# A fused attention and feed-forward kernel: low parts last in the first m-tile, two blocks in halves, another VectorE order in the bursts, a split last store

## The chip, the cores and the metric

The kernel runs on one core of a Trainium2 chip. The metric is device time in microseconds (us) from start to end of one execution; lower is better. The engines are called as the profile calls them: PE is TensorE (matmuls; PEld its weight loads), DVE is VectorE, ACT is ScalarE, POOL is GpSimd, SP is SyncE, which issues the DMAs.

## The reference

```python
# q, k, v: (8, 8, 576, 64) f32; attention inside chunks of 64 rows
scores = 1/sqrt(64) * q_c @ k_c.T            # per batch, head, chunk
attn   = exp(scores - max); attn = attn / (sum(attn) + 1e-9)
x      = (attn @ v_c) -> (4608, 512)         # heads side by side
h      = x @ w_in                            # w_in (512, 2048)
g      = maximum(h, 0) + log1p(exp(-abs(h))) # softplus
out    = g @ w_out                           # w_out (2048, 512), out (4608, 512) f32
```

## The kernel before

**Tiles.** The 4608 rows are 36 tiles of 128 (two chunks of one or two batches); four tiles are an m-tile of 512 rows, so there are 9 m-tiles. The hidden width of 2048 is 16 blocks of 128 (fc). For each m-tile and block, `gemm1` (L558) makes a 128x512 PSUM tile of h: 12 matmuls. `sp_g` (L578, ACT) is the softplus into u, `sp_hi` (L582, ACT) rounds it to g_hi, `sp_lo` (L586, DVE or POOL) makes g_lo = u − g_hi, and `gemm2` (L592) adds its product with w_out to four PSUM tiles: 12 matmuls. That is 9 × 16 × 2 = 288 groups of 12.

**Parts.** Each f32 operand is split into a high part, rounded to fp32r, and a low rest. A product is three matmuls: low times high, high times low, high times high, in that order before (L568, L601). The weights come as raw f32; per unit u (512 columns of w_in or w_out, 32 units) a DMA (`load`), a cast of the top (`w_top`, ACT or POOL), a scaled copy of the bottom (`w_low`, ACT), an addition (`w_add`, DVE), the high cast (`w_hi`, ACT or POOL) and the subtraction (`w_lo`, DVE or POOL) make the two parts.

**Attention.** The first four tiles (blocks 0 to 3) go through transposes on PE (`pe_t`, `pe_s`, `pe_e`, `pe_v`). From block 4 on two blocks go at a time, in 17 **bursts**: a burst (L550) does for each of two blocks the product with v of the pair before (`blk_v`, L532) and the scores of the next pair (`blk_s`, L451), both into one two-bank PSUM buffer `pa`. There are two such buffers, and gemm1 uses them too: after a burst the next gemm1 needs the first burst buffer. A buffer is free when ACT has cast x's high part out of it (`att_xh`, L544), DVE has subtracted it for the low part (`att_xl`, L548), and DVE has taken the row maximum (`att_max`, L496) and subtracted it (`att_sub`, L501). Then exp (ACT), denominator, normalisation, a 32x32 transpose (`blk_e`) and a swap of quarters, by 8 DMAs on SP's queue (`blk_swap`) or by transposes of parts on DVE (`blk_e4`, blocks in SWAP_DVE). q and k are loaded either in 8 small DMAs each or in one or two (blocks in WHOLE); the second way needs 8 partial transposes per tensor on DVE (`blk_t4`) instead of one (`blk_t`).

**Order.** Each engine's instruction order is written by a planner, `Plan` (L34 to L144): every piece of work is a task with engine, assumed cost, needs, and an urgency; the planner simulates the engines and always takes the ready task with the lowest urgency number. `due(g)` = T0 + TG × g gives the urgencies of what block g needs. `needs` wait for the end of a task, `after` only for its issue. The costs steer only the order; on the chip the engines wait for each other's semaphores. PE's order is fixed (L800 to L808): gemm1 of a block, a burst if one stands at that block (BEGIN, BURST_AT), gemm2 of the block before. Block 0 of the first m-tile is done in two halves (HALVES = 1): tiles 0 and 1 ahead as `a0`, then tiles 2 and 3. `keep_warm` (L330) puts filler matmuls where the plan sees PE idle. At the end `evacuate` (L607) copies each of four 128x512 results to SBUF, in turn on ACT and DVE, and `store` (L614) writes it with a DMA on SP's queue.

## Time and profile before

| | us |
|---|---|
| median of 3 runs | 866.99 (866.23 to 867.52) |
| profiled execution, its own time | 869.51 |
| its span, first to last instruction | 867.7 |
| busy PE / DVE / ACT / POOL | 850.9 / 347.6 / 309.9 / 64.7 |

The page also cuts the span into 40 equal slices of 21.7 us, with busy tenths in each; 9 is 90% or more:

```profile
DVE  5999964333424161425232342334241614121111
ACT  4576744232423242424242332324232424232222
POOL 0564641000000000000000000000000000000000
```

PE is at 9 in all slices but three. DVE is at 9 from the second slice to the fifth, where weights, the first m-tile and the early attention blocks meet; POOL works in the first seven slices only.

### The profile page before, as it was taken

What the parts mean: (1) busy time and instruction counts of PE and PEld (TensorE: products, weight loads), DVE (VectorE), ACT (ScalarE), POOL (GpSimd) and SP (SyncE); (2) the same over time, 40 slices, a digit from 0 to 9 for tenths busy, and PEclk for the clock granted to TensorE, in tenths of its full rate; (3) what the DMA queues carried; (4) which work ended last, traced back from release to release, by engine and by line L of the source; (5) the groups of instructions that cost most, each with busy time, mean ns of one, the idle gap of its engine ahead of it and who ended that gap; (6) DMA issues with size and microseconds to landing.
All of it is one profiled execution on the core that took longest, in us unless ns stands there. A gap on an engine that the chain in (4) does not pass through costs nothing.

```text
span 867.7 us, 14820 instructions
## 1 busy us (share of the span) xinstructions
PE 850.9 (98%) x5874; PEld 701.5 (81%) x5874; DVE 347.6 (40%) x589; ACT 309.9 (36%) x483; POOL 64.7 (7%) x68
## 2 busy tenths in 40 slices
PE   8799999999999999999999999999999999999998
PEld 7677878888888888888888888888888888888886
DVE  5999964333424161425232342334241614121111
ACT  4576744232423242424242332324232424232222
POOL 0564641000000000000000000000000000000000
PEclk9999999999999999999999999999999999999999
DMA  9787763312242224131332223122422241000001
GB/s 225 189 213 211 181 152 86 68 38 52 42 100 40 53 40 108 33 66 28 72 74 49 48 45 98 40 51 42 100 39 55 39 103 37 18 22 27 1 1 48
DMA packets 209957, 63.65 MB, mean 73 GB/s; under 512 B 187104, under 2 KB 203232, under 8 KB 209888
## 3 DMA queue, kind: packets, MB, share of 16 engines
q1 hardware_dynamic: 209888, 62.71, 31.8%
q8 instruction: 46, 0.75, 0.4%
q14 instruction: 23, 0.19, 0.1%
HBM read 45.09 MB, written 9.44 MB: 63 GB/s over the span
## 4 chain that ended last, share of the span: by engine, by line
PE 88%; DMA 5%; DVE 4%; ACT 1%; issue 1%; SPq 1%; POOL 0%; DVEq 0%; POOLq 0%; ACTq 0%
PE pa L569 42%; PE po L602 42%; DMA raw<-in_moe_w_out_dram 3%; PE pa L532 2%; PE pa L451 1%; DMA raw<-in_moe_w_in_dram 1%; DMA eT<-ka 1%; DVE wib L263 1%; PE po L332 1%; DVE g_lo L588 0%; SPq L324 0%; ACT u L580 0%; DVE mx L496 0%; DVE low L263 0%; DMA k<-in_v_dram 0%
## 5 line engine op out<-in xcount | busy, mean ns | idle before, releaser
L580 ACT ACTIVATE u<-pa 128x512 f32<-128x512 f32 (+1 forms) x145 | 86.2, 594 | 500.3 <-PE pa L569 500.2
L569 PE MATMUL pa<-x,wib 128*128 128x512 f32 x864 | 208.1, 390 | 0.3
L588 DVE TENSOR_TENSOR g_lo<-u,g_hi 128x512 fp32r<-128x512 f32 (+1 forms) x137 | 95.2, 695 | 280.1 <-ACT g_hi L584 276.6
L569 PEld LDWEIGHTS pa<-x,wib 128*128 128x128 f32 x864 | 161.7, 188 | 36.0 <-PE po L602 2.6
L569 PE MATMUL pa<-x,wi_hi 128*128 128x512 f32 (+1 forms) x584 | 178.8, 388 | 2.1 <-DVE x L548 2.1
L602 PE MATMUL po<-late,g_hi 128*128 128x512 f32 x540 | 169.5, 390 | 0.0
L569 PEld LDWEIGHTS pa<-x,wi_hi 128*128 128x128 f32 x584 | 109.8, 189 | 24.3 <-DVE x L548 2.3
L602 PEld LDWEIGHTS po<-late,g_hi 128*128 128x128 f32 x540 | 101.2, 188 | 21.3 <-issue 0.5
L569 PE MATMUL pa<-x,wi_lo 128*128 128x512 f32 (+1 forms) x292 | 113.8, 390 | 1.6 <-POOL top L249 1.0
L602 PE MATMUL po<-wo_hi,g_lo 128*128 128x512 f32 x288 | 113.4, 394 | 0.0
L602 PE MATMUL po<-late,g_lo 128*128 128x512 f32 x288 | 113.0, 392 | 0.0
L602 PE MATMUL po<-wo_lo,g_hi 128*128 128x512 f32 x288 | 112.4, 390 | 0.0
L602 PE MATMUL po<-wo_hi,g_hi 128*128 128x512 f32 x288 | 112.4, 390 | 0.0
L584 ACT CAST g_hi<-u 128x512 fp32r<-128x512 f32 (+1 forms) x145 | 89.5, 618 | 4.4
L569 PEld LDWEIGHTS pa<-x,wi_lo 128*128 128x128 f32 x292 | 55.1, 189 | 15.3 <-PE po L602 3.3
L602 PEld LDWEIGHTS po<-wo_hi,g_lo 128*128 128x128 f32 x288 | 54.3, 189 | 11.7
L602 PEld LDWEIGHTS po<-late,g_lo 128*128 128x128 f32 x288 | 54.1, 188 | 11.6
L602 PEld LDWEIGHTS po<-wo_hi,g_hi 128*128 128x128 f32 x288 | 54.2, 188 | 11.3
L602 PEld LDWEIGHTS po<-wo_lo,g_hi 128*128 128x128 f32 x288 | 54.3, 189 | 10.9
L496 DVE TENSOR_REDUCE mx<-pa 128x8 f32<-128x512 f32 x32 | 21.9, 685 | 68.5 <-ACT x L544 68.0
L428 DVE STREAM_TRANSPOSE qe<-q 128x512 f32<-128x512 f32 x29 | 20.5, 705 | 70.6 <-DMA k<-in_k_dram 55.2
L428 DVE STREAM_TRANSPOSE ka<-k 128x512 f32<-128x512 f32 x29 | 20.6, 711 | 53.0 <-DMA k<-in_k_dram 33.5
(101 smaller groups left out, 564.1 us busy)
## 6 DMA issues: line engine op xcount, KB each, us to landing
out_dram<-raw SPq DMA_DIRECT2D x36, 256.0 KB, 2.4
raw<-in_moe_w_in_dram SPq DMA_DIRECT2D x16, 512.0 KB, 4.9
raw<-in_moe_w_out_dram SPq DMA_DIRECT2D x16, 512.0 KB, 5.1
eT<-ka SPq DMA_DIRECT2D x248, 32.0 KB, 1.9
q<-in_q_dram SPq DMA_DIRECT2D x232, 32.0 KB, 2.1
k<-in_k_dram SPq DMA_DIRECT2D x232, 32.0 KB, 2.1
q<-in_v_dram SPq DMA_DIRECT2D x60, 64.0 KB, 2.5
k<-in_v_dram SPq DMA_DIRECT2D x60, 64.0 KB, 2.5
```

The lines of the kernel that those rows point to most:

```text
L263: nc.vector.tensor_tensor(low, low, live.pop(("top", u)), op=ALU.add)
L332: nc.tensor.matmul(dst[:, :P], ident, ident, start=True, stop=True)
L428: nc.vector.transpose(t, live.pop((n, i)))
L451: nc.tensor.matmul(pa[o, c2, col : col + C], qT[r, a * HP + hl, :], kT[r, a * HP + hl, :], start=True, stop=True,)
L496: nc.vector.tensor_reduce(mx, sc, axis=AX.X, op=ALU.max)
L532: nc.tensor.matmul(pa[o, a, col : col + C], vt[r, 4 * j + 2 * h2 + c2, :], eT[r, :, 4 * c2 + 2 * j + h2, :], start=True, stop=True,)
L569: nc.tensor.matmul(ph, wt[:, c, fs], x[:, ts_, c, :], start=(n == 0), stop=(n == 3 * KC - 1))
L580: nc.scalar.activation(w["u"], w["ph"], AF.Softplus)
L584: nc.scalar.copy(w["hi"], w["u"])
L588: (nc.gpsimd if pool else nc.vector).tensor_tensor(w["lo"], w["u"], w["hi"].bitcast(F32), op=ALU.subtract)
L602: nc.tensor.matmul(pos[w["m"]][t], gg[:, ts_], wt, start=(w["first"] and n == 0), stop=(w["last"] and n == 2),)
```

## The change

1. In the first m-tile (m < 1) gemm1 and gemm2 do all high-times-high matmuls of a group first, then the other two kinds; later m-tiles keep the three kinds side by side, high times high first. The planner is told by `late` that w_lo, x_lo and g_lo are needed only later in such a group.
2. HALVES = 2: blocks 0 and 1 of the first m-tile are done in halves.
3. In a burst `max` is planned to follow its block's x high cast; the second block's max, and the second x subtraction, follow the issue of the first block's score subtraction.
4. The last 128x512 result is copied in two halves of 256 columns, on ACT and DVE, and stored by two DMAs, one on ACT's queue, one on SP's.
5. The planner's costs and its lists of what runs where are other numbers, so the order of the first m-tile is another; the bursts stand at blocks 5 and 13 of an m-tile instead of 6 and 14, and weight loads follow the issue of v3's load instead of v0's.

```diff
@@ Plan.add, Plan.order
+        late={}
-                r = max(r, fin[n] + lat)
+                r = max(r, fin[n] + lat - t["late"].get(n, 0.0))
...
@@ gemm1
-        n = 0
-        for c in range(KC):
-            for wt, x in ((wi_lo, x_hi), (wi_hi, x_lo), (wi_hi, x_hi)):
-                nc.tensor.matmul(
-                    ph, wt[:, c, fs], x[:, ts_, c, :], start=(n == 0), stop=(n == 3 * KC - 1)
-                )
-                n += 1
+        terms = ((wi_hi, x_hi), (wi_lo, x_hi), (wi_hi, x_lo))
+        order = [(c, t) for t in terms for c in range(KC)] if w["m"] < 1 else [(c, t) for c in range(KC) for t in terms]
+        for n, (c, (wt, x)) in enumerate(order):
+            nc.tensor.matmul(ph, wt[:, c, fs], x[:, ts_, c, :], start=(n == 0), stop=(n == 3 * KC - 1))
@@ gemm2
-        for j, t in enumerate(w["tiles"]):
-            ts_ = slice(j * P, (j + 1) * P)
-            for n, (gg, wt) in enumerate(((g_lo, w_hi_), (g_hi, w_lo_), (g_hi, w_hi_))):
-                nc.tensor.matmul(
-                    pos[w["m"]][t], gg[:, ts_], wt,
-                    start=(w["first"] and n == 0), stop=(w["last"] and n == 2),
-                )
+        terms = ((g_hi, w_hi_), (g_hi, w_lo_), (g_lo, w_hi_))
+        tiles = list(enumerate(w["tiles"]))
+        order = [(n, j) for n in range(3) for j in tiles] if w["m"] < 1 else [(n, j) for j in tiles for n in range(3)]
+        for n, (j, t) in order:
+            nc.tensor.matmul(
+                pos[w["m"]][t], terms[n][0][:, j * P : (j + 1) * P], terms[n][1],
+                start=(w["first"] and n == 0), stop=(w["last"] and n == 2),
+            )
@@ new
+    def last_half(w, j):
+        m, t = w["m"], TPM - 1
+        cols = slice(j * DM // 2, (j + 1) * DM // 2)
+        o = live["out", m, t // 2][:, DM + cols.start : DM + cols.stop].bitcast(F32)
+        (nc.vector.tensor_copy if j else nc.scalar.copy)(o, pos[m][t][:, cols])
+        (nc.sync if j else nc.scalar).dma_start(out[m * MT + t * P : m * MT + (t + 1) * P, cols], o)
@@ the lists
-    HALVES = 1
+    HALVES = 2
...
-    T0, TG = 28.0, 5.5
+    T0, TG = 14.0, 5.5
...
-    WHOLE = (4,7)
-    SWAP_DVE = (7,)
+    WHOLE = (4,7,9)
+    SWAP_DVE = (4,7,9)
-    TOP_ACT = (0,3,8,9,11,15,16,17,20,21,25,26,29)
-    LOAD_AFTER = "v0"
-    LO_POOL = (0,2,6,9,10,12,17,18,23,25,29,31)
-    NORM_POOL = (3,5,6,7)
-    GLO_POOL = (4,6,9,10,12,15,17,18)
+    TOP_ACT = (0,1,4,5,6,7,8,11,15,17,20,21,24,25,26,28,29,30)
+    LOAD_AFTER = "v3"
+    LO_POOL = (0,2,3,4,5,6,7,12,17,18,19,20,26,27,28,30,31)
+    NORM_POOL = (1,2,4,7)
+    GLO_POOL = (0,3,5,7,8,9,10,11,14,15,16)
-    BURST_AT = (6, 14)
+    BURST_AT = (5, 13)
-    V_AFTER = "load16"
-    K6_AFTER = "load10"
-    QK_URG = 30
+    V_AFTER = "load8"
+    K6_AFTER = "load13"
+    QK_URG = 0
-    V_URG = -5
-    SW_URG = 0
-    EXP_FROM = 1
+    V_URG = 20
+    SW_URG = 40
+    EXP_FROM = 3
...
@@ the bursts
-                plan.add(f"xl{i}", "DVE", 0.65, partial(att_xl, i), [f"xh{i}"], urg=d)
+                plan.add(f"xl{i}", "DVE", 0.65, partial(att_xl, i), [f"xh{i}"], urg=d + 0.5 * n,
+                         after=[f"sub{2 * ps}"] if n and ps is not None else [])
-            plan.add(f"max{i}", "DVE", 0.65, partial(att_max, i), [f"B{at}_{n}"], urg=d)
-            plan.add(f"sub{i}", "DVE", 0.65, partial(att_sub, i), [f"max{i}"], urg=d)
+            first = [f"B{at}_{n}"] if bursts[at][0] is None else [f"xh{2 * bursts[at][0] + n}"]
+            plan.add(f"max{i}", "DVE", 0.68, partial(att_max, i), first, urg=d + 0.2 * n,
+                     after=[f"sub{a}"] if n else [])
+            plan.add(f"sub{i}", "DVE", 0.68, partial(att_sub, i), [f"max{i}"], urg=d + 0.2 * n)
...
@@ the tasks of gemm1 and gemm2
+            slow = {f"w_lo{of_in[fc]}": 0.9 * part, **{f"xl{m * TPM + t}": 1.8 * part for t in w["tiles"]}}
+        slow = {f"w_lo{of_out[fc]}": 0.9 * part, f"lo{name}": 1.8 * part} if m < 1 else {}
...
@@ the last result
+                if m == NM - 1 and t == TPM - 1:
+                    for j in range(2):
+                        plan.add(f"ev{m}_{t}" + "ab"[j], "DVE" if j else "ACT", 0.4, partial(last_half, w, j), [f"G2_{g}"],
+                                 urg=-3, after=[f"ev{m}_{t - 1}"])
+                    continue
```

## Rows read from the trace of the kernel before

**Rows 1.** The page's chain that ended last, shares of the span by engine.

```profile
PE 88%; DMA 5%; DVE 4%; ACT 1%; issue 1%; SPq 1%; POOL 0%; DVEq 0%; POOLq 0%; ACTq 0%
```

**Rows 2.** Stages: stretch, its length, busy us (instructions) by engine, clock, DMA share, GB/s.

```profile
core 0: us, PE busy (x) PEld busy (x) DVE busy (x) ACT busy (x) POOL busy (x), PEclk, DMA share, GB/s
25.49:27.16 1.67, 1.67 (x12) 1.47 (x12) 1.60 (x5) 1.65 (x4) 0.60 (x1) 1.00 1.04 272
27.16:33.83 6.67, 3.45 (x54) 3.00 (x53) 6.60 (x11) 4.68 (x8) 4.22 (x5) 1.00 0.66 146
33.83:38.16 4.33, 4.33 (x17) 3.92 (x18) 4.24 (x8) 1.48 (x3) 0.87 (x3) 0.61 0.64 133
38.16:50.50 12.34, 12.34 (x56) 9.96 (x54) 11.54 (x20) 7.29 (x12) 6.74 (x8) 1.00 0.73 203
50.50:80.90 30.40, 29.11 (x185) 23.48 (x185) 27.78 (x47) 19.95 (x31) 16.74 (x17) 1.00 0.78 211
80.90:122.85 41.95, 41.85 (x296) 34.02 (x296) 33.65 (x49) 25.48 (x41) 23.82 (x24) 1.00 0.73 193
```

**Rows 3.** Timeline of one steady burst, all engines: start, us, engine, line, what.

```profile
208.18 2.88 PE L569 MATMUL pa<-x,wib 128*128 128x512 f32 x12
...
211.73 0.62 ACT L584 CAST g_hi<-u 128x512 fp32r<-128x512 f32 x1
...
212.87 0.69 DVE L496 TENSOR_REDUCE mx<-pa 128x8 f32<-128x512 f32 x1 [5.23 <-ACT x L544]
...
213.04 0.50 PE L602 MATMUL po<-late,g_lo 128*128 128x512 f32 x1
...
213.47 0.68 DVE L588 TENSOR_TENSOR g_lo<-u,g_hi 128x512 fp32r<-128x512 f32 x1
...
214.07 1.28 DVE L548 TENSOR_TENSOR x<-pa,x 128x512 fp32r<-128x512 f32 x2
...
215.27 0.68 DVE L501 TENSOR_TENSOR qe<-pa,mx 128x512 f32<-128x512 f32 x1
...
216.10 2.99 PE L569 MATMUL pa<-x,wib 128*128 128x512 f32 x12
...
218.92 0.39 PE L602 MATMUL po<-late,g_lo 128*128 128x512 f32 x1
```

**Rows 4.** PE's timeline at the second, third and fourth burst.

```profile
77.13 2.88 PE L569 MATMUL pa<-x,wib 128*128 128x512 f32 x12
...
84.27 0.50 PE L602 MATMUL po<-wo_hi,g_lo 128*128 128x512 f32 x1
...
120.04 2.88 PE L569 MATMUL pa<-x,wib 128*128 128x512 f32 x12
...
126.39 0.50 PE L602 MATMUL po<-late,g_lo 128*128 128x512 f32 x1
...
161.88 0.39 PE L569 MATMUL pa<-x,wi_lo 128*128 128x512 f32 x1
...
167.25 0.50 PE L602 MATMUL po<-wo_hi,g_lo 128*128 128x512 f32 x1
...
170.10 0.39 PE L569 MATMUL pa<-x,wi_lo 128*128 128x512 f32 x1
...
172.82 0.39 PE L602 MATMUL po<-wo_hi,g_lo 128*128 128x512 f32 x1
```

**Rows 5.** Who waited: weight loads, line, releaser, us in total, times, longest.

```profile
PEld pa L569 <- PE po L602: 5.9, 13, 0.7
```

**Rows 6.** DVE's groups up to 124 us, shapes apart: count, busy us, mean ns.

```profile
L588 DVE TENSOR_TENSOR g_lo<-u,g_hi 128x512 fp32r<-128x512 f32 x9 | 8.8, 977 | 0.8 <-ACT g_hi L584 0.7
...
L438 DVE STREAM_TRANSPOSE ka<-k 32x256 f32<-32x256 f32 x8 | 3.5, 436 | 0.1
```

**Rows 7.** Timeline near the first burst, POOL and DVE.

```profile
52.65 1.29 POOL L288 TENSOR_TENSOR wo_lo<-wib,wo_hi 128x512 fp32r<-128x512 f32 x1
...
52.75 1.73 DVE L588 TENSOR_TENSOR g_lo<-u,g_hi 128x512 fp32r<-128x512 f32 x1
```

**Rows 8.** Timeline at the end: the last copy.

```profile
864.05 0.69 DVE L611 COPY raw<-po 128x512 f32<-128x512 f32 x1 [0.67 <-PE po L602]
```

More of the change, by code (lines that the diff above doesn't have):

```diff
@@ L49, in add @@
     def add(
-        self, name, eng, cost, fn, needs=(), urg=0.0, table=None, take=(), kb=0, slack=0.0, after=(), port=False, parts=1
+        self, name, eng, cost, fn, needs=(), urg=0.0, table=None, take=(), kb=0, slack=0.0, after=(), port=False, parts=1,
+        late={}
     ):
@@ L53, in add @@
             name=name, eng=eng, cost=cost, fn=fn, needs=list(needs) + list(after), after=set(after), urg=urg, table=table,
-            take=take, kb=kb, slack=slack, seq=len(self.tasks), port=port or eng == "POOL", parts=parts,
+            take=take, kb=kb, slack=slack, seq=len(self.tasks), port=port or eng == "POOL", parts=parts, late=late,
         )
@@ L120, in order @@
                         dma_free = max(end + 1.0, dma_free) + t["kb"] * 1024 / self.RATE / t["parts"]
-                        lanes.append(max(dma_free + 0.7, end + 1.8))
+                        lanes.append(max(dma_free + 0.8, end + 1.8))
                     last = lanes[-1]
@@ L680, in chunked_attention_softplus_ffn @@
         plan.add(f"load{u}", "POOL" if pool else "SP", 0.75 if pool else 0.55, partial(w_load, u, is_in, fc),
-                 urg=d - LEAD if u else LQ, kb=480,
+                 urg=d - LEAD if u else LQ, kb=504,
                  take=[("raw", [f"w_top{u}", f"w_low{u}"])], after=[LOAD_AFTER])
@@ L764, in chunked_attention_softplus_ffn @@
                 two = 1 + (2 * i // NCH != (2 * i + 1) // NCH)
-                plan.add(f"{n}{i}", "SP", 0.55 * two if whole else 4.2, partial(blk_load, i, n, src), free,
+                plan.add(f"{n}{i}", "SP", 0.55 * two if whole else 4.6, partial(blk_load, i, n, src), free,
                          urg=d - QK_URG, kb=310 if whole else 430, parts=two if whole else 8,
@@ L769, in chunked_attention_softplus_ffn @@
                 if whole:
-                    plan.add(f"U{n}{i}", "DVE", 1.6, partial(blk_t4, i, n, 0), [f"{n}{i}"] + keep, urg=d - T_URG)
-                    plan.add(f"T{n}{i}", "DVE", 1.6, partial(blk_t4, i, n, 1), [f"U{n}{i}"], urg=d - T_URG)
+                    plan.add(f"U{n}{i}", "DVE", 1.76, partial(blk_t4, i, n, 0), [f"{n}{i}"] + keep, urg=d - T_URG)
+                    plan.add(f"T{n}{i}", "DVE", 1.76, partial(blk_t4, i, n, 1), [f"U{n}{i}"], urg=d - T_URG)
                 else:
@@ L789, in chunked_attention_softplus_ffn @@
             if i in SWAP_DVE:
-                plan.add(f"Tf{i}", "DVE", 1.6, partial(blk_e4, i, 0), [f"norm{i}"] + gone, urg=d)
-                plan.add(f"Te{i}", "DVE", 1.6, partial(blk_e4, i, 1), [f"Tf{i}"], urg=d)
+                plan.add(f"Tf{i}", "DVE", 1.76, partial(blk_e4, i, 0), [f"norm{i}"] + gone, urg=d)
+                plan.add(f"Te{i}", "DVE", 1.76, partial(blk_e4, i, 1), [f"Tf{i}"], urg=d)
                 swapped[i] = f"Te{i}"
@@ L794, in chunked_attention_softplus_ffn @@
                 plan.add(f"Te{i}", "DVE", 0.65, partial(blk_e, i), [f"norm{i}"], urg=d)
-                plan.add(f"swap{i}", "SP", 4.4, partial(blk_swap, i), [f"Te{i}"] + gone, urg=d - SW_URG, kb=190, parts=8)
+                plan.add(f"swap{i}", "SP", 4.8, partial(blk_swap, i), [f"Te{i}"] + gone, urg=d - SW_URG, kb=190, parts=8)
                 swapped[i] = f"swap{i}"
@@ L814, in chunked_attention_softplus_ffn @@
         needs += [f"xl{m * TPM + t}" for t in w["tiles"]]
-        plan.add(f"G1_{name}", "PE", 2.78 if part == 1 else 1.5, partial(gemm1, w), needs, urg=1e6, take=[("pa", [f"sp{name}"])])
+        slow = {}
+        if m < 1:
+            slow = {f"w_lo{of_in[fc]}": 0.9 * part, **{f"xl{m * TPM + t}": 1.8 * part for t in w["tiles"]}}
+        plan.add(f"G1_{name}", "PE", 2.72 if part == 1 else 1.44, partial(gemm1, w), needs, urg=1e6, take=[("pa", [f"sp{name}"])],
+                 late=slow)
         plan.add(f"sp{name}", "ACT", 0.1 + 0.5 * part, partial(sp_g, w), [f"G1_{name}"], urg=-2, table="softplus",
@@ L822, in chunked_attention_softplus_ffn @@
         take = [("po", [f"ev{m}_{t}"]) for t in w["tiles"]] if w["first"] else []
-        plan.add(f"G2_{name}", "PE", 2.78 * part, partial(gemm2, w),
+        slow = {f"w_lo{of_out[fc]}": 0.9 * part, f"lo{name}": 1.8 * part} if m < 1 else {}
+        plan.add(f"G2_{name}", "PE", 2.72 * part, partial(gemm2, w),
                  [before[f"G2_{name}"], f"lo{name}", f"w_lo{of_out[fc]}", f"w_hi{of_out[fc]}"], urg=1e6, take=take,
-                 after=[f"S{FIRST_BLK - 1}"] if m == 0 and w["first"] else [])
+                 after=[f"S{FIRST_BLK - 1}"] if m == 0 and w["first"] else [], late=slow)
         if w["last"]:
@@ L828, in chunked_attention_softplus_ffn @@
                 odd = t % 2
+                if m == NM - 1 and t == TPM - 1:
[3 more added lines that the diff above has]
+                    continue
                 plan.add(f"ev{m}_{t}", "DVE" if odd else "ACT", 0.65, partial(evacuate, w, t), [f"G2_{g}"], urg=-3,
-                         take=[] if odd else [("raw", [f"st{m}_{t}", f"st{m}_{t + 1}"])],
+                         take=[] if odd else [("raw", [f"st{m}_{j}" for j in (t, t + 1) if m < NM - 1 or j < TPM - 1])],
                          after=[f"ev{m}_{t - 1}"] if odd else [])
```

12 lines of the change are left out of this document (6 added, 6 removed).

## The prediction, made before the kernel was run

> **What bounds the kernel now.** I read the chain of waits first, then a table of busy time by stage, then the TensorE timeline around the bursts, and last VectorE's instructions in the first 124 us. The chain gives TensorE 88% of the span [rows 1]: the kernel is a queue of matmul groups, and only time in which that queue stands still or runs slowly can be won. A group of twelve 512-column matmuls takes 2.72 us (172.82 − 170.10) [rows 4]. 288 of them are 783.4 us, the same before and after; the other 84 us of the 867.7 us span are attention bursts, the start, and waits.
>
> Steady state first [rows 3]. After a burst the next L602 group starts at 213.04, the next L569 group at 216.10 and the L602 group after it at 218.92: 3.06 and 2.82 us. After the burst at 164.69 the same two steps are 2.85 and 2.72 [rows 4]. A burst period is 16 groups and (218.92 − 208.18) − 3 × 2.72 = 2.58, so 46.10 us, of which a steady burst loses (3.06 + 2.82) − (2.85 + 2.72) = 0.31 us. The L569 group at 216.10 needs the burst's first PSUM buffer, and VectorE frees that last: max at 212.87, g_lo at 213.47, both x subtractions at 214.07, and only at 215.27 the score subtraction, over at 215.95. The list of waits has this stall 13 times [rows 5]: the first burst and 12 steady ones.
>
> Then the start [rows 2]. From 27.16 to 122.85 VectorE is busy 6.60 of 6.67, 4.24 of 4.33, 11.54 of 12.34, 27.78 of 30.40 and 33.65 of 41.95 us, idle 11.9 us in all, of which only 3.6 before the second burst. TensorE is busy 3.45 of the 6.67 us before 33.83, partly with filler, and in the next 4.33 us its granted clock is 0.61 on average, part of it at 1.2 GHz, right after the engine had been little used. Two early bursts are long: from the L569 group's start to the next L602 group, less 2.72, the second takes 84.27 − 77.13 − 2.72 = 4.42 us and the third 126.39 − 120.04 − 2.72 = 3.63, against 213.04 − 208.18 − 2.72 = 2.14 in the steady state [rows 3, 4].
>
> **The change part by part.**
>
> *VectorE's order in a burst.* Now the max is added as following its block's hi copy, which is what the trace does anyway (212.87, released by ACT's x copy) [rows 3], the second x subtraction comes only after the first score subtraction, and the second max after it too. g_lo is ready at about 212.4 and goes first, then first x subtraction, max, score subtraction. Four instructions at the 0.60 to 0.69 spacing of rows 3 from 212.4 end at about 215.1. TensorE wants the buffer at 213.04 + 2.85 = 215.89, so 0.8 us is spare and the 0.31 goes. Twelve times: **3.7 us**. The second buffer is freed two to three instructions later, but it is wanted a further 5.44 us on. If g_lo ended as late as a blocked one, 1.73 us [rows 7], the release would be at about 216.1 and most would stay; but from the eighth of the 40 slices on GpSimd does nothing (the page), so I take the whole 3.7.
>
> *Bursts at blocks 5 and 13 instead of 6 and 14.* The number of bursts is unchanged; the later ones keep their spacing. Only the third-to-fourth gap shrinks, by one block (5.44 us). The fourth burst waited before: from 161.88 to 167.25, less 2.72, is 2.65, 0.51 over steady. On its side are block 9's swap, now four-part transposes on VectorE instead of eight DMAs on SP, and exps no longer held behind the following block's hi. Against it stands the 5.44. Bounds +5 and −0.5; I take the wait as gone, **0.5 us**.
>
> *Low parts last, halves, and the re-planned first m-tile.* The number of matmuls of an unsplit block is the same. One more block is split: twelve 256-column matmuls took at most 1.67 us [rows 2], so two halves cost between 0 and 0.6 more than 2.72; I take 0.2. What can be won: (a) the slow clock: 4.33 us held 11 narrow and 6 wide matmuls, worth 11 × 0.12 + 6 × 0.227 = 2.7, so 1.6; (b) in 27.16 to 33.83 TensorE has room for the second ahead half and the first L602 half, two halves of 2.72, so 2.7 us; (c) the first three bursts: at most 0.7 (first, its L569 group waits for the score subtraction, no longer than the 0.7 of rows 5), 4.42 − 2.14 = 2.3 and 3.63 − 2.14 = 1.5. Together 8.8.
>
> VectorE must feed it. By the lists, two tensors of block 9 are newly transposed in eight pieces each (8 × 0.436 = 3.5 [rows 6] less 0.7, twice: +5.6) and block 4's swap too (+2.8); five w_lo (0.68) and four g_lo (0.69) go to GpSimd (−6.2): +2.2 us net up to the third burst. GpSimd's longer list also blocks: the nine g_lo on VectorE took 977 ns on average there [rows 6] against 0.68 free [rows 3], 0.3 more; for about ten more GpSimd instructions 3 us. So of 11.9 idle some 6.7 are left, and only 3.6 lie ahead of the second burst. The nearest limit is that one: I take **3.5 us** net of the 0.2, with 0 and 8.8 as ends. Five more tops go from GpSimd to ACT, under 1 us each, 5 us at most, which ACT's idle time hides: 30.40 − 19.95 before and 41.95 − 25.48 after the second burst [rows 2]. Covers that may fail: weight loads now wait for all of q, k and v of the first four blocks on SP's queue, which starts the weights later by up to three v loads.
>
> About that block: the Trainium skill, "SBUF — State Buffer", section "SBUF: two separate sides", has VectorE and GpSimd share one pair of ports under an exclusive lock held for a whole instruction. The trace agrees: g_lo started at 52.75 beside a GpSimd subtraction of 52.65 to 53.94 and took 1.73 us [rows 7]; by it each moved subtraction could cost VectorE up to 1.04 us, which is the slower rival's price below.
>
> *Last store in two halves.* The last copy is 0.69 us after 864.05 [rows 8]. A half is about 0.35 to 0.4. In parallel: −0.3. One after the other: +0.1. ACT's queue has nothing else left, and the second DMA runs beside the first. I take 0, ends −0.4 and +0.3.
>
> That a PSUM bank is not read by two engines at once is the rule of the Trainium skill, "PSUM — Partial Sum Buffer", section "PSUM bank collisions raise a hardware error". The trace agrees as far as the max at 212.87 waits for ACT's copy out of the same buffer [rows 3]; by it the two last halves run one after the other and the tail is the +0.1.
>
> **Sum.** 3.7 + 0.5 + 3.5 = 7.7 off the profiled span of 867.7 (its own time 869.51, 1.8 more). The median of the runs, 866.99, is 2.5 below that own time; the waits are the same work in both, so I take 7.7 off the median: **859.3 us**. Own range 856 to 862.
>
> **Rivals.**
> *All of the early time is won* (8.8 instead of 3.5): 866.99 − 3.7 − 0.5 − 8.8 = 854.0. For it: 8.3 of VectorE's idle time lies before the third burst. Against: 3.6 before the second. Chance 0.15.
> *Nothing early is won*: the halves only shift the wait onto weights that VectorE makes no sooner. 866.99 − 4.2 = 862.8. For it: VectorE 97% busy up to 50.50. Against: five w_lo and four g_lo leave it. 0.20.
> *The order doesn't do what it says*: VectorE's queue still ends the score subtraction after 215.9. 866.99 − 0.5 − 3.5 = 863.0. 0.06.
> *Slower*: VectorE blocked behind GpSimd before the third burst. 5.6 + 2.8 of transposes, nine moved subtractions each blocking 1.04 (9.4), less 6.2: 11.6 us more. If only the 3.6 idle before the second burst can take any of it, the third burst is 8.0 late: 866.99 + 8.0 − 4.2 = 870.8. It decides from a lateness of 4.2, that is from 7.8 us more on VectorE. For it: rows 7. Against: the mean block is 0.3, not 1.04. 0.07.
> The forecast has 0.52.
>
> **Range and chances.** 0.2%, about what a measurement tells from no change, is 1.7 us: 865.3 and 868.7. Low end: all won, 854.0. High end: 862.8 plus one more stretch at the slow clock (1.6) and a late fourth burst (0.5), 865.0. Outside lie the slower rival and a little at both ends, about 0.15. Faster: forecast, both early rivals and the third rival, less a tenth for bad combinations: 0.86; within 0.2% 0.07; slower 0.07.
>
> **What would show it.** In the steady state the L569 group after a burst starts 2.85 us after the L602 group, the score subtraction ends before it is wanted, and bursts are 45.8 us apart instead of 46.1. The L569 stall of rows 5 is gone from the list. The first full-rate group comes some 2 to 4 us sooner than 38.16 [rows 2] for the same work done, the clock in that stretch is higher, and VectorE's g_lo mean up to the third burst is not far above 977 ns. The prediction is wrong if the spacing stays 46.1, if the third burst comes later than before for the same block count, or if the fourth waits for a swap or a v load.

## The result, and the profile after

The changed kernel is 0.3% slower: 869.81 us (median; 869.06 to 871.29) against 866.99, ratio 1.0031 (95% interval 1.0018 to 1.0044); a second series, a0, gave 870.63, 1.0028 (1.0014 to 1.0043). Forecast was 859.3. The profiled execution has a span of 868.0 and an own time of 869.81.

35 runs of the kernel before spread from 865.6 to 870.4 us. Its two profiles differ only ahead of the fourth burst: from the group ahead of that burst to the end they take 705.8 and 706.0 us. The execution that the prediction read (span 867.7, own time 869.51) was a long one, and a second profile of that kernel, b0_again (span 865.4, own time 867.18, 0.7 below the median of its series), is the better base. Below, "before" is that second profile unless rows are named.

The chain of the changed kernel, which answers to [rows 1], is as full of TensorE as it was:

```profile
PE 88%; DVE 3%; DMA 2%; SPq 2%; ACT 2%; POOL 1%; issue 1%; DVEq 0%; ACTq 0%; POOLq 0%
```

The steady state is what was forecast. Timeline of one steady burst of the changed kernel, answering to [rows 3]:

```profile
205.01 2.88 PE L570 MATMUL pa<-x,wib 128*128 128x512 f32 x12
...
209.21 0.69 DVE L586 TENSOR_TENSOR g_lo<-u,g_hi 128x512 fp32r<-128x512 f32 x1 [4.74 <-ACT g_hi L582]
209.82 0.68 DVE L549 TENSOR_TENSOR x<-pa,x 128x512 fp32r<-128x512 f32 x1
209.87 0.74 PE L601 MATMUL po<-late,g_hi 128*128 128x512 f32 x2
...
210.42 0.68 DVE L497 TENSOR_REDUCE mx<-pa 128x8 f32<-128x512 f32 x1
...
211.13 0.69 DVE L502 TENSOR_TENSOR qe<-pa,mx 128x512 f32<-128x512 f32 x1
...
212.72 2.88 PE L570 MATMUL pa<-x,wib 128*128 128x512 f32 x12
...
215.44 0.62 PE L601 MATMUL po<-late,g_hi 128*128 128x512 f32 x2
```

g_lo, first x subtraction, max, score subtraction: the first buffer is free at 211.82, 0.9 us ahead of the group that wants it. L601 to L570 takes 2.85 us and L570 to L601 2.72, in place of 3.06 and 2.82; bursts are 45.79 us apart. The stall of [rows 5] is gone from the list of waits.

The loss lies ahead of the fourth burst. Stages of the changed kernel, busy us and count by engine, answering to [rows 2]:

```profile
core 0: us, PE busy (x) PEld busy (x) DVE busy (x) ACT busy (x) POOL busy (x), PEclk, DMA share, GB/s
21.65:28.47 6.82, 6.14 (x82) 5.27 (x78) 5.18 (x12) 4.78 (x9) 1.97 (x2) 0.50 0.73 116
...
27.16:33.83 6.67, 5.40 (x85) 4.61 (x80) 5.33 (x11) 4.46 (x8) 3.13 (x3) 0.90 0.90 261
33.83:38.16 4.33, 4.32 (x31) 3.83 (x29) 4.17 (x10) 3.44 (x8) 2.05 (x2) 1.00 0.45 82
38.16:50.50 12.34, 10.67 (x51) 8.78 (x52) 7.50 (x12) 9.35 (x17) 9.27 (x9) 1.00 1.04 290
50.50:80.90 30.40, 30.34 (x240) 24.73 (x242) 29.50 (x52) 17.80 (x28) 18.00 (x19) 1.00 0.82 206
80.90:122.85 41.95, 38.43 (x247) 30.59 (x236) 39.67 (x65) 30.18 (x47) 24.80 (x23) 1.00 0.60 171
```

Full clock comes sooner, as hoped (1.00 from 33.83 on, where [rows 2] have 0.61). But the stretch at the lower level (granted clock 0.50, that is 1.2 GHz) is no shorter: it is 6.82 us long and lies further ahead, while 0.61 on average over 4.33 us amounts to 3.4; and in a0 the clock is at 0.50 once more from 41.2 to 44.6. VectorE has 86.2 us of work in the five stretches from 27.16 on, 2.4 more than the 83.8 of [rows 2]; the forecast had 2.2. But its idle time has moved: 4.84 us of it now lie between 38.16 and 50.50, where TensorE stands still for 1.7, and of the 8.3 us that were idle ahead of the third burst 2.3 are left. From the group ahead of the second burst to the group ahead of the third, VectorE is busy 43.2 of 46.0 us; before it was 35.9 of 41.4. TensorE's timeline in the changed kernel, answering to [rows 4] (in brackets the idle time before a group and what ended it):

```profile
39.13 0.73 PE L601 MATMUL po<-wo_hi,g_hi 128*128 128x512 f32 x2 [0.98 <-ACT wo_hi L285]
...
40.56 0.73 PE L601 MATMUL po<-wo_lo,g_hi 128*128 128x512 f32 x2 [0.70 <-POOL wo_lo L289]
...
48.49 1.07 PE L570 MATMUL pa<-x,wi_hi 128*128 128x512 f32 x4
...
77.30 2.88 PE L570 MATMUL pa<-x,wib 128*128 128x512 f32 x12
...
83.64 0.69 PE L452 MATMUL pa<-ka,qe 64*64 64x64 f32 x30 [1.50 <-DVE ka L439]
...
105.44 2.11 PE L570 MATMUL pa<-x,wib 128*128 128x512 f32 x8 [0.50 <-DVE wib L289]
...
112.47 2.11 PE L570 MATMUL pa<-x,wib 128*128 128x512 f32 x8 [1.29 <-DVE wib L289]
...
123.30 1.19 PE L570 MATMUL pa<-x,wib 128*128 128x512 f32 x4 [0.52 <-POOL wib L285]
...
159.24 0.39 PE L570 MATMUL pa<-x,wi_hi 128*128 128x512 f32 x1
...
166.93 0.39 PE L570 MATMUL pa<-x,wi_hi 128*128 128x512 f32 x1
```

And the kernel before, second profile, at the same places:

```profile
48.35 0.39 PE L569 MATMUL pa<-x,wi_lo 128*128 128x512 f32 x1
...
77.19 2.88 PE L569 MATMUL pa<-x,wib 128*128 128x512 f32 x12
...
85.99 2.88 PE L569 MATMUL pa<-x,wib 128*128 128x512 f32 x12
...
118.63 2.88 PE L569 MATMUL pa<-x,wib 128*128 128x512 f32 x12
```

At the group ahead of the first burst the two are level (48.49 and 48.35), and at the group ahead of the second still (77.30 and 77.19). What the start had won was spent by the first burst, and two waits for the parts of w_out, at 39.13 and 40.56, are 1.7 us of it. Then the kernel before runs six pairs of groups (one gemm1, one gemm2) without a wait, (118.63 − 85.99) / 6 = 5.44 us each, and the changed one waits in its second burst for block 7's k in pieces, and in three groups for weights. The group ahead of the third burst starts at 123.30 against 118.63. That group is the mark used below ("mark"). Six profiles with the early order of before put it between 118.6 and 121.0 (median 119.8), three of the changed kernel's between 121.8 and 124.4 (median 123.3). So a single mark is good to about 1.3 us either way, this pair of profiles shows more of a difference (4.67) than the medians (3.5), and verdicts rest on the median times.

The end of the changed kernel, all engines, answering to [rows 8]:

```profile
862.21 0.39 PE L601 MATMUL po<-late,g_lo 128*128 128x512 f32 x1
862.63 0.37 ACT L621 COPY raw<-po 128x256 f32<-128x256 f32 x1
863.03 0.38 ACTq L622 DMA_DIRECT2D out_dram<-raw  x1
863.04 0.42 DVE L621 COPY raw<-po 128x256 f32<-128x256 f32 x1 [1.07 <-ACT raw L621]
863.49 0.33 SPq L622 DMA_DIRECT2D out_dram<-raw  x1
863.87 0.94 SPq L615 DMA_DIRECT2D out_dram<-raw  x2
```

The halves run one after the other, and the second half's DMA stands on SP's queue ahead of the stores of tiles 1 and 2, whose results were ready earlier. They go out at 863.87; from the last matmul to the end it is 868.0 − 862.6 = 5.4 us, before 865.4 − 861.7 = 3.7.

Between the two profiles the account closes. A burst's excess is counted here from the gemm1 group ahead of it to the next gemm1 group, less the 5.44 us of a pair. Start to mark +4.67, third burst (3.28 in place of 2.72) +0.56, fourth burst (166.93 − 159.24 − 5.44 = 2.25 for 2.94) −0.69, the steady bursts −3.65 as measured, end +1.7: +2.6, as the spans differ.

### The profile page after: what moved, and what is told of

It reads as the page before. It is cut to its first block, busy times and chain, and to the rows that moved or that the text cites. A ratio compares the mean times of both kernels' runs of the same rounds, so it can differ in the third digit from the quotient of the medians.

```text
span 868.0 us, 14833 instructions
## 1 busy us (share of the span) xinstructions
PE 849.0 (98%) x5890; PEld 702.5 (81%) x5890; DVE 352.6 (41%) x610; ACT 315.8 (36%) x494; POOL 69.9 (8%) x70
## 4 chain that ended last, share of the span: by engine, by line
PE 88%; DVE 3%; DMA 2%; SPq 2%; ACT 2%; POOL 1%; issue 1%; DVEq 0%; ACTq 0%; POOLq 0%
PE po L601 42%; PE pa L570 42%; PE pa L533 2%; PE pa L452 2%; SPq L316 2%; DMA raw<-in_moe_w_out_dram 1%; DMA raw<-in_moe_w_in_dram 1%; DVE qe L439 1%; DVE low L264 1%; DVE ka L439 1%; POOL late L289 0%; PE pa L333 0%; DVE wib L289 0%; ACT u L578 0%; ACT top L250 0%
## 5 line engine op out<-in xcount | busy, mean ns | idle before, releaser
L586 DVE TENSOR_TENSOR g_lo<-u,g_hi 128x512 fp32r<-128x512 f32 (+1 forms) x135 | 93.1, 689 | 452.6 <-ACT g_hi L582 448.0
L570 PE MATMUL pa<-x,wib 128*128 128x512 f32 x864 | 208.7, 390 | 3.1 <-DVE wib L289 2.4
L570 PEld LDWEIGHTS pa<-x,wib 128*128 128x128 f32 x864 | 161.8, 188 | 38.6 <-DVE wib L289 3.7
L570 PE MATMUL pa<-x,wi_hi 128*128 128x512 f32 (+1 forms) x592 | 186.1, 383 | 0.0
L601 PE MATMUL po<-late,g_hi 128*128 128x512 f32 x540 | 166.3, 391 | 0.0
L570 PEld LDWEIGHTS pa<-x,wi_hi 128*128 128x128 f32 x592 | 109.6, 188 | 22.1
L601 PEld LDWEIGHTS po<-late,g_hi 128*128 128x128 f32 x540 | 100.7, 188 | 21.1
L601 PE MATMUL po<-wo_hi,g_hi 128*128 128x512 f32 x288 | 109.7, 393 | 1.0 <-ACT wo_hi L285 1.0
L601 PE MATMUL po<-wo_lo,g_hi 128*128 128x512 f32 x288 | 108.7, 390 | 0.7 <-POOL wo_lo L289 0.7
L570 PE MATMUL pa<-x,wi_lo 128*128 128x512 f32 (+1 forms) x296 | 108.6, 383 | 0.0
L601 PE MATMUL po<-wo_hi,g_lo 128*128 128x512 f32 x288 | 108.5, 389 | 0.0
L601 PE MATMUL po<-late,g_lo 128*128 128x512 f32 x288 | 108.2, 389 | 0.0
L601 PEld LDWEIGHTS po<-wo_lo,g_hi 128*128 128x128 f32 x288 | 54.0, 188 | 12.1 <-POOL wo_lo L289 1.1
L601 PEld LDWEIGHTS po<-wo_hi,g_hi 128*128 128x128 f32 x288 | 53.7, 188 | 12.4 <-ACT wo_hi L285 1.2
L570 PEld LDWEIGHTS pa<-x,wi_lo 128*128 128x128 f32 x296 | 54.7, 188 | 10.9
L601 PEld LDWEIGHTS po<-wo_hi,g_lo 128*128 128x128 f32 x288 | 54.1, 188 | 11.3
L601 PEld LDWEIGHTS po<-late,g_lo 128*128 128x128 f32 x288 | 54.1, 188 | 11.3
L513 DVE TENSOR_REDUCE den<-qe 128x8 f32<-128x512 f32 x32 | 21.1, 659 | 16.3 <-ACT qe L508 16.3
L549 DVE TENSOR_TENSOR x<-pa,x 128x512 fp32r<-128x512 f32 x36 | 24.5, 683 | 3.6 <-ACT x L545 3.6
```

Source lines behind the costliest of these rows:

```text
L513: nc.vector.tensor_reduce(den, e, axis=AX.X, op=ALU.add)
L549: nc.vector.tensor_tensor(lo, live.pop(("xp", i)), hi.bitcast(F32), op=ALU.subtract)
L570: nc.tensor.matmul(ph, wt[:, c, fs], x[:, ts_, c, :], start=(n == 0), stop=(n == 3 * KC - 1))
L586: (nc.gpsimd if pool else nc.vector).tensor_tensor(w["lo"], w["u"], w["hi"].bitcast(F32), op=ALU.subtract)
L601: nc.tensor.matmul(pos[w["m"]][t], terms[n][0][:, j * P : (j + 1) * P], terms[n][1], start=(w["first"] and n == 0), stop=(w["last"] and n ...
```

## Experiments

**The base, and the burst order alone.** b0_again is the kernel before. b3 has only VectorE's new order, from the fourth burst on, so that nothing ahead is planned anew; b3_again is the same.

```diff
+ nw = ps > F + 2
- "xl{i}" urg=d;  "max{i}" needs B{at}_{n}
+ "xl{i}" urg=d + 0.5*n*nw, after=[sub{2*ps}] if n and nw
+ "max{i}" needs xh{...} if nw, urg=d + 0.2*n*nw, after=[sub{a}] if n and nw
```

> The kernel before, unchanged, for a trace on the same chip as the other runs of this call. Theory A (the profile of before that was read ahead of the prediction was a slow execution of an otherwise steady kernel): ratio 1.000, median near 867, and the trace's first burst stands about 2 us earlier than 50.5. Theory B (the two kernels differ by only 0.3 us, as the two profiles' spans do, and the runs' medians came from different conditions): median near 869.

> Before, with the new order of max, subtractions and x subtractions on DVE in the bursts from the fourth on, and nothing else of the change; up to the fourth burst every engine's order is that of before. Theory A (0.31 us in each of 12 steady bursts): 3.7 us faster, ratio 0.9957, bursts 45.8 us apart. Theory B (part of it is given back elsewhere): 46.1 apart or ratio above 0.998.

> The kernel before with VectorE's order in the bursts from the fourth on, once more, beside the control: 864.0 to 865.2, 0.9960 to 0.9975 of before.

b0_again: 867.91, ratio 1.0005 (0.9993 to 1.0017). b3: 864.55, 0.9966 (0.9955 to 0.9976); again 864.43, 0.9963 (0.9949 to 0.9977). The bursts of b3 are 45.8 us apart. This part of the change is worth about 3.1 us on its own, the 3.7 of the forecast within the interval, and it is the fastest version found that computes what the reference does.

**The last store whole** (a1), and **the matmul order of before inside the groups** (a2), each in the changed kernel with nothing else planned anew.

```diff
# a1: the last result by one copy and one DMA
- for j in range(2): plan.add("ev8_3" + "ab"[j], ..., last_half)
# a2
- order = all c of one term, then the next   (m < 1)
+ order = all three terms of one c, then the next c
```

> After, with the last 128x512 result copied whole by DVE and stored by one DMA, as before. Theory A (the half's DMA stands in SP's queue ahead of the stores of tiles 1 and 2 and holds them until the last copy is done): the stores go out as soon as their copies end, the time from PE's end to the span's end falls from 5.4 to 3.7 us, ratio 1.0011, some 1.6 us below the changed kernel. Theory B (the halves cost nothing, the late end is an instruction fetch): stays at the changed kernel's 869.8, ratio 1.003.

> After, with the matmuls inside each group in the order of before (low parts first, the three kinds side by side); every engine's order of groups and instructions otherwise the same. Theory A (low parts last does save waits in the first m-tile): slower than the changed kernel by 1 to 4 us, ratio 1.005 to 1.008, with longer waits of PE for w_lo and g_lo. Theory B (the waits only move inside the group, since the next group has the same producers): within 0.5 us of the changed kernel, ratio 1.003.

> The changed kernel, unchanged, beside the single undoings of this call. All theories: ratio 1.003 (1.002 to 1.004), bursts 45.8 apart, third burst's group (block 15) starting at 121.5 to 123.5 where before on the same chips has 118.6.

a1: 868.64, 1.0013 (1.0002 to 1.0024), and its end is 865.0 − 861.4 = 3.6 us after the last matmul: the split costs 1.3 to 1.6 us by the ratios, whose intervals overlap, and 1.8 by the ends in the profiles. a2: 869.42, 1.0016 (1.0004 to 1.0028), against 1.0031 and 1.0028 for the changed kernel: taking out "low parts last" costs nothing.

**Single lists of the plan undone** (a4, a5, a6). Each plans the whole first m-tile anew.

```diff
# a4
- WHOLE = (4,7,9)
+ WHOLE = (4,7)
# a5: LO_POOL and GLO_POOL as before
# a6
- LOAD_AFTER = "v3"
+ LOAD_AFTER = "v0"
```

> After, with block 9's q and k loaded in 8 small DMAs each and one whole transpose, as before (its swap stays on DVE). Theory T1 (the 16 partial transposes of q9 and k9, 7.0 us of DVE between the second and the third burst, push the w_lo that PE waits for): DVE busy there falls from 39.8 of 42 us to about 35, PE's waits for DVE in that stretch (some 3 us) go, 3 to 4 us faster than the changed kernel, ratio about 0.999. Theory T2 (DVE is held up by GpSimd's longer list) or T3 (weights loaded late): less than 1 us, ratio 1.002 or above.

> After, with w_lo and g_lo on GpSimd or DVE as in the lists of before (9 of them back on DVE up to the third burst). T2 (each GpSimd subtraction blocks DVE): w_lo on DVE in 78 to 128 us falls from 1.4 us to 0.9 on average, 2 to 4 us faster than after, ratio about 1.000. T1 (DVE is simply full): slower than after by 2 to 6 us, ratio 1.005 to 1.010, since 6.2 us of work comes back to a full engine. T3: within 1 us.

> After, with the weight loads allowed from the issue of v0's load, as before, instead of v3's. T3 (weights come 4 to 5 us late, so that DVE stands idle for 4.8 of 12 us between 38 and 50 and does that work later, in the full stretch): DVE idle in 38 to 50 falls below 2 us, first L570 group from 30.9 to some 27, 2 to 4 us faster than after, ratio about 1.000. T1 or T2: within 1 us of after.

All are slower than the changed kernel: 871.99 (1.0059; 1.0038 to 1.0080, which still touches the changed kernel's interval), 874.0 (1.0078), 882.15 (1.0163). In a4 VectorE did fall from 40.0 to 33.2 busy us between 80 and 122, but the mark stayed at 124.18 behind a new wait of 2.20 us for POOL's high half. Nothing follows about single lists: an undone list leaves the others fitted to its old value.

**The written order kept, one operation made shorter or moved.** f4 moves block 6's swap behind two weight loads on SP's queue; f2 transposes block 7's k whole; f24 is both; f5 transposes block 9's q and k whole; f6 is all three; f7 lets GpSimd write low halves of weights as copies. In all of these but f4 a part of the work is left out: a whole transpose doesn't give the layout that the scores need, and a copy leaves the high part in the low one. They serve for the time alone.

```diff
# f4, in emit(): move "swap6" behind "load26"
+ seq.insert(at.index("load26"), seq.pop(at.index("swap6")))
# f2 (i == 7 and n == "k"), f5 (i == 9), f6 (both, and f4), in blk_t4
+ if ...:
+     if c2 == 0: blk_t(i, n)      # one 128x512 transpose for eight pieces
+     return
# f7, in w_lo
- nc.gpsimd.tensor_tensor(lo, t, hi, op=ALU.subtract)
+ nc.gpsimd.tensor_copy(lo, t)
```

> The changed kernel with one step of its written order moved and nothing planned anew: the eight transfers of block 6's swap stand on SP's queue behind the weight loads 25 and 26 in place of in front of them (the kernel before has them behind load 26 too). In the changed kernel the queue stands from 89.8 to 95.5 us waiting for that swap's transpose and gives the swap's transfers out until 100.4, and loads 25 and 26 go out at 100.5 and 101.2, where the kernel before gives them out at 95.8 and 96.3. Theory Q (the queue order holds the weight stream, and that is the part of the loss which the groups 12 to 15 show): loads 25 and 26 go out near 90 us, their additions on VectorE come 3 to 5 us sooner, the waits of L570's groups for w_lo and w_hi before the third burst (2.9 us) mostly go, the group ahead of the third burst begins at 121 to 122 in place of 123.3 to 124.4, and the time is 867.3 to 868.3. Rival V (what binds there is the work as a whole, VectorE's and the transfers', whatever its order on SP): the group begins at 123.5 or later and the time is 869.3 to 871.

> The changed kernel, its order unchanged, with one full-width transpose of block 7's k on VectorE in place of its eight partial ones (so block 7's scores are not those of the reference): 0.67 us of VectorE in place of 3.6, just ahead of the second burst. Theory D (the second burst's wait of 1.50 us for these pieces is lost for good): the second burst is over its ideal by 3.3 us in place of 4.8, every later group comes 1.5 us sooner, and the time is 868.3 to 869. Theory Q (from there to the third burst the weight stream sets the pace): the wait in the second burst goes, but the groups 12 to 15 wait so much longer for w_lo and w_hi, the group ahead of the third burst stays within 0.7 us of 123.3 to 124.4, and the time is 869.3 to 870.5.

> Both edits in one: block 6's swap behind loads 25 and 26 on SP's queue, and block 7's k transposed whole (its scores then not the reference's). If the early loss is these two (1.5 us in the second burst and 2.9 us in the groups from 12 to 15): the group ahead of the third burst begins at 119 to 120.5, as in the kernel before (118.6), and the time is 865.5 to 867. If the stage is held by its work as a whole: 122 or later and 868.5 to 870.

> The changed kernel, its order unchanged, with one full-width transpose each of block 9's q and k on VectorE in place of eight partial ones each (block 9's scores are then not the reference's): 1.3 us of VectorE in place of 7.1, between 108 and 121 us. Theory R (from 105 us to the third burst the ring of the two buffers low, by ScalarE's low part, VectorE's addition, the high and the low half, is held by VectorE, which stands full with these transposes): the additions 28 to 31 come 2 to 4 us sooner, the group ahead of the third burst begins at 120 to 121.5 in place of 123.0 to 124.4, the time is 867 to 868.2. Rival G (the ring is held by GpSimd's halves, or by the transfers): the group begins within 0.7 us of 123.0, the time is 869.3 to 870.5. The version planned anew without these pieces had come no sooner; this one changes no order.

> The changed kernel with three edits and no new plan: block 7's k and block 9's q and k transposed whole (their scores not the reference's), block 6's swap behind loads 25 and 26 on SP's queue. With the two of them without block 9 the group ahead of the third burst began at 122.2 and the time was 868.3. Theory R: 119.3 to 120.7 and 865.8 to 867.2, that is the early loss is made of VectorE's pieces. Rival G: 121.7 or later and 868 to 869.

> The changed kernel, its order unchanged, with GpSimd writing the low halves of weights as plain copies of the sum and not as differences (so the low weights of these units are not the reference's): some 0.6 to 1.0 us in place of 1.3 to 1.7 for each, and an operation with one input, not two. Rival G (GpSimd's longer differences, and what they do to VectorE beside them, hold the ring): the group ahead of the third burst begins at 120 to 121.5, the time is 867 to 868.2. Theory R (VectorE's pieces hold it): within 0.7 us of 123.0 to 124.4, the time is 869 to 870.5.

| | us | ratio to before (interval) | mark |
|---|---|---|---|
| changed kernel, two series | 869.81, 870.63 | 1.0031, 1.0028 | 123.3, 124.4 |
| f4 | 869.5 | 1.0026 (1.0015 to 1.0036) | 123.0 |
| f2 | 868.76 | 1.0013 (1.0000 to 1.0025) | 122.1 |
| f24 | 868.34 | 1.0011 (1.0000 to 1.0021) | 122.2 |
| f5 | 868.94 | 1.0013 (1.0004 to 1.0021) | 122.4 |
| f6 | 867.65 | 0.9997 (0.9987 to 1.0007) | 121.4 |
| f7 | 866.23 | 0.9978 (0.9969 to 0.9987) | 119.6 |

Theory Q (SP's queue) fell: loads 25 and 26 went out 4.5 us sooner than in a0, at 96.0 and 96.7, but the additions that need them came only 0.4 and 1.1 us sooner (107.43 against 107.85, 109.82 against 110.90), and the time did not move measurably. The low part that the first of them needs waited for a buffer, not for data: in a0, 0.82 us for one of VectorE's differences. Theory D fits (868.76, forecast 868.3 to 869): the 1.5 us in the second burst are 1 to 1.6 us of the time, with intervals that overlap. f5 falls between the forecasts of theory R and its rival, worth 1.3 to 1.6 us, with intervals that barely overlap. All three edits together give 2.7 to 3.0 us (0.0031 to 0.0034), clear of the intervals. Rival G, which a5 seemed to have ruled out, is the largest: 4.3 to 4.6 us (0.0050 to 0.0053), more than its own forecast, and the mark is back among those of before. These gains can't be added, since the edits shorten links of one chain.

The chain behind the wait at 123.30, in the changed kernel, all engines:

```profile
111.96 1.60 POOL L289 TENSOR_TENSOR late<-low,late 128x512 fp32r<-128x512 f32 x1
112.45 1.80 DVE L439 STREAM_TRANSPOSE qe<-q 32x256 f32<-32x256 f32 x4
...
113.59 0.66 ACT L259 ACTIVATE low<-raw 128x512 int32<-128x512 uint32 x1 [3.96 <-POOL late L289]
...
116.52 1.30 POOL L289 TENSOR_TENSOR wib<-low,wib 128x512 fp32r<-128x512 f32 x1 [2.96 <-ACT wib L285]
...
117.77 1.30 POOL L289 TENSOR_TENSOR late<-low,late 128x512 fp32r<-128x512 f32 x1
117.89 1.73 DVE L586 TENSOR_TENSOR g_lo<-u,g_hi 128x512 fp32r<-128x512 f32 x1
...
119.21 0.68 ACT L259 ACTIVATE low<-raw 128x512 int32<-128x512 uint32 x1
...
119.65 1.80 DVE L439 STREAM_TRANSPOSE ka<-k 32x256 f32<-32x256 f32 x4
...
121.48 1.29 DVE L264 CUSTOM_DVE_ANT_0 low<-low,top 128x1024 uint16<-128x1024 uint16 x2
...
122.24 1.01 POOL L285 CAST wib<-low 128x512 fp32r<-128x512 f32 x1 [3.16 <-DVE low L264]
...
123.30 0.97 PE L570 MATMUL pa<-x,wib 128*128 128x512 f32 x3 [0.52 <-POOL wib L285]
```

There are two buffers named low, which hold the weights of one unit each while they are split. ScalarE may write the next low part only when GpSimd's difference has read the last one (3.96 us of waiting at 113.59, and another low part right after GpSimd's difference of 117.77 to 119.07); then VectorE has to add, and it stands behind four pieces of block 9's k (119.65 to 121.45) before its two additions; then GpSimd makes the high half, and TensorE starts. Each link is short; the chain goes around through three engines, and a long link on any of them delays the next lap. In f7 the same links on GpSimd, and ScalarE's high half beside the second of them:

```profile
108.82 1.07 POOL L290 CAST late<-low 128x512 fp32r<-128x512 f32 x1
...
112.02 1.01 POOL L290 CAST wib<-low 128x512 fp32r<-128x512 f32 x1 [2.14 <-DVE low L264]
...
112.17 0.61 ACT L285 CAST wib<-low 128x512 fp32r<-128x512 f32 x1
...
112.99 0.61 POOL L290 CAST late<-low 128x512 fp32r<-128x512 f32 x1
```

1.07, 1.01 and 0.61 us in place of 1.60, 1.30 and 1.30, and the lap starts some 3 us sooner. The copy differs from the difference in three ways. It is shorter; with it VectorE's next subtraction was not held (the g_lo of 117.89 took 1.73 us, the one in its place in f7 0.69); and it does not read the high half, so it need not wait for it (at 116.52 the difference had waited 2.96 us for ScalarE's high half, at 112.02 the copy starts ahead of it). f7 changes all three at once and does not say which counts.

a5 had given these differences back to VectorE, which then was busy 39.6 of the 42 us between 80 and 122, but it is a plan of its own. The Trainium skill, "Perfetto Trace Analysis", section "Optimizing Scalar/DVE Operations", warns that moving work between VectorE and GpSimd may not help, since they share a port. The runs agree as far as neither side was the better one here: with more of the differences on GpSimd 1.0031, with fewer, in a5's plan, 1.0078. How much of it is the port was not separated.

**The control to f7** (g7): the same edit on b3.

> The kernel before with VectorE's order in the bursts from the fourth on (864.55 alone), and GpSimd writing the low halves of its ten weight units as plain copies and not as differences (so these low weights are not the reference's); the control to the same edit on the changed kernel, which has fifteen such units there and gained about 4 us by it. If the differences on GpSimd bind only in the newly planned order: the group ahead of the third burst stays within 0.7 us of 118.6 to 119.5, and the time is 0 to 1 us below that of the same kernel with differences in this call. If they bind in either order: the group comes 2 us or more sooner, and the time is 2 to 3 us below.

863.79, 0.9960 (0.9944 to 0.9976), against 864.43 (0.9963; 0.9949 to 0.9977) for b3 beside it. With the early order of before, copies in place of GpSimd's differences give 0.3 to 0.6 us, within the noise of about 1.8; with the new one 4.3 to 4.6. (The edit touches twelve units there and seventeen here, not ten and fifteen.) The mark of g7, 117.8, is earlier than the six of before, but its profiled execution was also among the fastest of its six, 862.28; so a small gain there is not excluded. By the list of waits, ScalarE's writes into the low buffers waited 5.6 us for transfers in the kernel before, 2.1 for VectorE's differences and never for GpSimd's; in the changed one they waited 4.3 us for GpSimd's differences and 4.4 for VectorE's, and in f7 2.8 for GpSimd's copies.

**Parts carried to the early order of before.** c2 is b3 with low parts last; d1 is b3 with the bursts at 5 and 13 and the last result in halves, the second half's store as a task of its own behind the other stores.

```diff
# c2: the matmul loops of the changed kernel in gemm1 and gemm2
# d1
- BURST_AT = (6, 14)
+ BURST_AT = (5, 13)
+ plan.add("st8_3b", "SP", ..., urg=2e5)   # behind st8_1 and st8_2
```

> The kernel before with two parts of the change: VectorE's order in the bursts from the fourth on (alone 864.55) and the low parts last in the products of the first m-tile, with the early order of before. If low parts last are worth something only where the order is not planned for it: nothing or little, 864.0 to 865.0, as taking them out of the changed kernel had given nothing. If they give the groups room by themselves (the burst at the third place waits less for w_lo): 862.5 to 863.8. This is the version that may beat both.

> The kernel before with what the runs have shown to be good of the change: the new order of VectorE's work in the bursts from the fourth on, these bursts one group earlier (at 5 and 13), and the last result in two halves, the second half's store behind the other stores on SP's queue. Its written order up to the fourth burst is that of the kernel before. The burst order alone had 864.55. Bursts one group earlier: the fourth burst 0.5 us shorter. Tail: the stores of the tiles 1 and 2 no longer wait for VectorE's last copy as in the changed kernel, so the end comes 3.3 to 3.8 us after the last matmul, as before: -0.4 to 0. Sum 863.6 to 864.5. If the positions matter in another way (loads of the next blocks meet the bursts): 864.5 to 866.

c2: 866.02, 0.9974 (0.9963 to 0.9984): no better than b3. The matmuls do come sooner, the group ahead of the second burst at 75.4 against 77.3 in b3, and then wait for what has not moved, in the second burst for v and in the third for ScalarE; behind the first of these waits the granted clock is 0.50 from 81.0 to 84.4:

```profile
80.05 1.58 PE L532 MATMUL pa<-eT,x 64*64 64x64 f32 x29 [1.81 <-DMA x<-in_v_dram]
...
125.92 0.69 PE L532 MATMUL pa<-eT,k 64*64 64x64 f32 x32 [2.14 <-ACT u L577]
```

d1: 872.15, 1.0056 (1.0034 to 1.0078), a miss of 8 us. One group earlier, the fourth burst meets v loads that have not landed; from TensorE's timeline of d1:

```profile
160.22 0.29 PE L532 MATMUL pa<-eT,q 64*64 64x64 f32 x2 [1.44 <-ACT g_hi L584]
160.91 0.34 PE L532 MATMUL pa<-eT,q 64*64 64x64 f32 x6 [0.41 <-DMA q<-in_v_dram]
...
166.11 0.81 PE L532 MATMUL pa<-eT,k 64*64 64x64 f32 x19 [1.12 <-DMA k<-in_v_dram]
```

The six waits in this burst are 3.9 us, five of them, 2.5 us, for v. The granted clock is 0.70 between 160 and 165 and 0.64 in the ten us behind, part of it at 1.2 GHz, after an engine that had mostly waited (2.2 of the 3.2 us ahead of 162). The burst's excess is 11.4 us, 8.8 more than in b3, in a profiled execution of 873.96, 1.8 above the median. Its end, in halves with the queue mended, is 872.2 − 868.5 = 3.7 us after the last matmul: as long as with one copy, so halves give nothing even then.

## Why the prediction was wrong

**VectorE's order in a burst: right.** Forecast 0.31 us twelve times, 3.7; alone it gives 3.0 to 3.2 us by the ratios of b3, and the mechanism is the one that was named.

**Bursts at 5 and 13: right in size, wrong as a separate part.** The fourth burst is 0.5 us shorter than in [rows 4] (an excess of 2.25 for 170.10 − 161.88 − 5.44 = 2.78). With the early order of before, d1 shows the opposite: there the position brings the case named as "if the fourth waits for a swap or a v load".

**Low parts last, halves and the re-planned first m-tile: the step that failed.** Taken as 3.5 us won, with 0 and 8.8 as ends; it is a loss of 5.2 us between the two profiles (4.67 + 0.56), and 4.1 by the times, a1 (868.64) against b3 (864.5), which differ in the early order and the positions alone. Of (a) and (b), the clock and the room before 33.83, only the first came, since the slow stretch lies ahead of the first group (in a0 not even that). TensorE's first half group starts at 30.90, not 25.49, so the room was not filled, and by the first burst nothing was left. The step counted VectorE as one sum over 27.16 to 122.85, and the sum came true (+2.4 for +2.2). Its fault was to take the place with the least idle time, before the second burst, as "the nearest limit". Idle time appeared there and vanished ahead of the third burst, where sixteen new pieces of block 9 and GpSimd's differences fall into the chain of the two low buffers. f7 shows what that chain is worth: with copies on GpSimd the changed kernel is at 0.9978, and less the 0.0015 to 0.0018 of the split store that is 0.9960 to 0.9963 (an estimate), level with b3. A bound of zero loss had no reason behind it: that an order with the same work can be later was left out.

Low parts last, by itself, is worth nothing measurable on either order (a2, c2). The halves of the second block were not run by themselves.

**Weight loads behind all of q, k and v**, named as a cover that may fail: the first group comes later (30.90 us, [rows 2] have it at 25.49), but a plan with the earlier loads was worse (a6), and it is another plan as a whole, so the runs don't price it.

**Last store in two halves: mis-sized.** Taken as 0 with +0.3 as the upper end; it costs 1.3 to 1.8 us. The argument followed ACT's queue and missed SP's, on which the second half's DMA was written in front of two stores. The Trainium skill's rule on PSUM banks ("PSUM — Partial Sum Buffer", section "PSUM bank collisions raise a hardware error"), quoted in the prediction, agrees with the trace as far as VectorE's half starts only when ScalarE's is over (863.04, after 862.63 + 0.37); by it alone the tail would have been +0.1.

**The rivals.** The slower one gave 870.8 and the time is 869.8, but not by its mechanism as priced: VectorE has 2.4 us more to do, not 11.6, and its g_lo takes 894 ns on average up to 124 us, less than the 977 of [rows 6]. That the time came near is luck. GpSimd's differences do decide (f7), as links of a chain; whether by their own length, by what they take from VectorE beside them or by their wait for the high half is not separated. The other rivals ended on the faster side. (One reading there is off: VectorE is 96% busy up to 50.50 by [rows 2], not 97; nothing hangs on it.)

**Size.** The excess was taken from a single profile, and a long one: by the prediction's count (to the next L602 group, less 2.72) the second and third burst have 4.42 and 3.63 in [rows 4], 3.23 and 2.57 in the second profile. With b3, its repeat and d1 that makes five profiles, with medians of 3.8 and 3.1. (c) had 2.3 and 1.5 to win there; by the medians it is 1.7 and 1.0.

What stays open: which list of the plan one would have to change to keep the early start without the loss. Freezing the order shows what binds, not what a planner would make of it.

## What to carry to other kernels

When a change re-plans a stage, balance each engine stretch by stretch, up to each point where TensorE needs something, and follow the chains that go around through few buffers: a sum over the stage can come true and the stage still be late. To find the cause afterwards, keep the written order and shorten one operation; undoing one list of a plan makes a third plan. A DMA that waits for a late copy belongs behind the stores that are ready, on the same queue or on another.

## What the runs showed of the hardware

Four partial transposes on VectorE took 1.80 us beside GpSimd's difference (112.45, beside 111.96 to 113.56), the same as elsewhere, while a g_lo that starts beside one took 1.73 in place of 0.69 (117.89): of VectorE's instructions only some are held. It is so in the whole trace of the changed kernel up to 130 us. 24 partial transposes start while GpSimd is at an operation with two inputs and take 0.43 to 0.44 us each, like the 35 that have none beside them (0.42 to 0.44); six subtractions with two inputs in SBUF start so and take 0.76 to 1.79 us, in place of 0.64 to 0.69 for eleven that have none beside them. The Trainium skill, "SBUF — State Buffer", section "SBUF: two separate sides", says that of VectorE's instructions those with two SBUF inputs, or in certain modes, meet the lock; both rows agree, the transpose having one input and the g_lo two.

The prediction priced blocking for every moved subtraction alike, whatever VectorE does beside it; transposes, the larger part of VectorE's new work, paid none here.
